# Gated mix of a spectral filter and a diagonal recurrence on one core: recurrence by token chunks, transforms split by parity, skip and gate on the matrix engine

## The chip, the cores and the metric

The kernel runs on 1 core of one Trainium2 chip. The time is the device time of one execution, in microseconds (us). Each kernel is run several times, and the profile is one of these executions. A run is called slow here when it took over 1.5% longer than the fastest run of the same kernel; comparisons of times use fast runs. TensorE (PE) does matmuls, which accumulate in a memory called PSUM. VectorE (DVE) does the elementwise work and scans, ScalarE (ACT) moves results from PSUM to the working memory SBUF (an eviction) and computes functions, GpSimd (POOL) does small odds and ends, SyncE (SP) issues transfers (DMA).

## The reference, cut to what matters

```python
# x: 2048 tokens x 1024 features, bf16
g = sigmoid((x * gate_w).sum(-1))                       # one gate per token
a = irfft2(rfft2(x) * (w_r + 1j * w_i))                 # spectral filter
Lam_bar = exp(dt * Lam)                                 # 1024 complex states
B_bar = ((Lam_bar - 1) / Lam)[:, None] * (B_re + 1j * B_im)
for t in range(2048):
    h = Lam_bar * h + B_bar @ x[t]                      # recurrence over tokens
    b[t] = 2 * real((C_re + 1j * C_im) @ h) + x[t] * Dskip
out = g * a + (1 - g) * b
```

The kernel takes the 2-D transform apart: a d transform (a real transform over the 1024 features, by matmul with a matrix of cosines and sines), two stages over the 2048 tokens (2048 = 128 x 16, with a turn through DRAM between them), the product with w, the two token stages back (with a second turn), and the inverse d transform. The recurrence is turned into a real one: u = B x is rotated by a table of angles, scanned with a real decay on VectorE, and rotated back. In other words there are two independent branches, spectral and recurrent, whose instructions are interleaved, and a final product with C that needs both.

## The kernel before

The x loads come first. G waits behind them in SP's queue (it is issued at 17.1 us, B's first transposed load at 30.1 us), and one of the four loads of T3 is held back by a one-element copy that reads the last transposed block of x; the other loads of T3, K3, R12, JP and the columns of w are issued from 1.2 us on:

```python
    for r in range(16):
        xn = CT[r // 8][:, r % 8, :]
        nc.sync.dma_start(out=xn, in_=x[P * r:P * (r + 1), :])
    for r in range(16):
        xn = CT[r // 8][:, r % 8, :]
        pe_transpose_block(xn, xT[:, :, P * r:P * (r + 1)], nc.vector.tensor_copy)
        gjunk = stg.tile([P, D], BF16, name="gjunk", tag="stg")
        nc.vector.scalar_tensor_tensor(out=gjunk, in0=xn, scalar=1.0, in1=gw_bc, ...,
                                       accum_out=glog[:, r:r + 1])        # the gate's sum
    # ...
    T3_sb = gconst.tile([P, 16, 3, P], BF16, name="T3_sb")
    nc.gpsimd.tensor_copy(out=T3_sb[:, 0, 0, 0:1], in_=xT[:, 7, S - 1:S])
```

The recurrence goes by blocks of 128 states, each over all four chunks of 512 tokens, and writes its result to DRAM:

```python
    def pass1(jb):
        # ... transposed loads of B's block, tables of angles ...
        for c in range(NCH):
            # 16 matmuls: psu = B x for 512 tokens; u <- psu on ScalarE
            nc.vector.tensor_mul(out=cu, in0=u, in1=tab[:, 0:1, :].to_broadcast([P, 2, TC]))
            nc.vector.tensor_mul(out=su, in0=u[:, ::-1, :], in1=tab[:, 1:3, :])
            nc.vector.tensor_add(out=v, in0=cu, in1=su)
            for ri in range(2):
                nc.vector.tensor_tensor_scan(out=g[:, ri, :], data0=rb, data1=v[:, ri, :], ...)
            # ... carry to the next chunk ...
            nc.sync.dma_start(out=h_dram[c, :, jb, :, :], in_=g)
```

The d transforms contract over all 1024 features, and over all 1024 frequencies on the way back:

```python
        def fd(j):
            for h in range(2):
                for dblk in range(8):
                    nc.tensor.matmul(ps[:, K * h:K * (h + 1)], lhsT=xT_A[:, dblk, j, :],
                                     rhs=G_sb[:, dblk, K * h:K * (h + 1)], ...)
    # ... and the inverse:
            for nh in range(2):
                for c in range(2):
                    for kc in range(4):
                        nc.tensor.matmul(psy[:, 512 * nh:512 * (nh + 1)], lhsT=ZT[:, kc, c, :],
                                         rhs=Ginv_sb[:, 4 * c + kc, 512 * nh:512 * (nh + 1)], ...)
```

The last stage reads the recurrence back, rotates it, multiplies by C, and mixes on VectorE:

```python
                # 32 matmuls: ps_y = h C for 128 tokens, then
                nc.vector.tensor_mul(out=sk, in0=xc, in1=dsk_bc)                   # x * Dskip
                nc.vector.scalar_tensor_tensor(out=pre, in0=sk, scalar=omg[:, tb:tb + 1], in1=gac, ...)
                nc.vector.scalar_tensor_tensor(out=o, in0=psy, scalar=omg[:, tb:tb + 1], in1=pre, ...)
```

## Time and profile before

| | before |
|---|---|
| median of 3 runs | 508.51 us (506.78 to 509.82) |
| span of the profiled run | 507.4 us |
| PE busy | 426.4 us |
| DVE busy | 350.6 us |
| ACT busy | 183.1 us |
| mean granted TensorE clock | 0.935 |

These are lines of the profile's page of the kernel before: the span, the busy time of each engine, and the chain of work that ended last, by engine and by line. In the two lines with tile names after them, a group of instructions is given with its count, busy time, mean nanoseconds of one, and the engine's idle time just before it.

```profile
span 507.4 us, 5763 instructions
PE 426.4 (84%) x2049; PEld 211.4 (42%) x2087; DVE 350.6 (69%) x633; ACT 183.1 (36%) x246; POOL 14.0 (3%) x21
...
DVE 37%; PE 36%; DMA 10%; issue 8%; ACT 7%; SPq 1%; DVEq 0%; ACTq 0%
...
L342 PE MATMUL ps_fd<-G_sb,xT 128*128 128x512 bf16 x250 | 63.5, 408 | 15.7 <-ACT X_766 L345 7.2
...
L514 PE MATMUL ps_id<-Ginv_sb,ZT 128*128 128x512 bf16 x255 | 57.9, 380 | 1.1 <-ACT ga L519 1.0
```

The two d transforms alone, ps_fd and ps_id, are 121 of the 426 us of PE. The shares of a whole run hide that the stages have different limits, so here is the kernel before cut into stretches of time. The columns are the stretch, its length, then busy us (and instructions) of PE, PEld, DVE, ACT and POOL, the granted clock, the DMA share and GB/s.

```profile
0.00:35.35 35.35, 14.39 (x133) 12.94 (x135) 27.86 (x48) 1.28 (x1) 10.93 (x18) 0.95 1.05 231
35.35:175.00 139.65, 121.69 (x521) 64.19 (x531) 81.63 (x164) 78.09 (x125) 3.08 (x4) 0.93 0.54 118
175.00:191.80 16.80, 4.80 (x19) 1.86 (x17) 9.47 (x14) 5.31 (x10) 0.00 (x0) 0.71 1.13 237
191.80:265.00 73.20, 69.29 (x374) 30.55 (x379) 69.07 (x179) 44.90 (x51) 0.00 (x0) 0.93 0.64 194
265.00:281.00 16.00, 10.01 (x41) 5.02 (x41) 14.23 (x24) 8.95 (x13) 0.00 (x0) 0.79 0.81 142
281.00:361.00 80.00, 78.53 (x409) 40.59 (x416) 35.54 (x56) 40.17 (x45) 0.00 (x0) 1.00 0.35 117
361.00:390.00 29.00, 20.59 (x85) 8.80 (x86) 20.42 (x32) 4.39 (x5) 0.00 (x0) 0.82 0.76 273
390.00:507.40 117.40, 107.06 (x477) 47.45 (x485) 92.43 (x120) 0.00 (x0) 0.00 (x0) 0.98 0.44 154
```

Read them in order: loading and transposing x; the forward transform with the recurrence; the first turn through DRAM; the filter; the second turn; the inverse; a wait for the end of the recurrence; the product with C. In the inverse PE is busy 78.5 of 80 us, so a matmul taken away there should come off the time. In the first turn it is busy 4.8 of 16.8.

Three pieces of the chain of work, in order of time (start us, length, what), show one row block of the inverse and, just as C starts, the write of the recurrence's last result and the load of the gated branch (gac) behind it in SP's queue:

```profile
301.27 3.51 PE ps_id L514 x16
...
385.50 2.27 DMA h_scratch<-g
...
388.24 7.31 DMA gac<-ga_scratch
```

### The profile page before, as it was taken

To read this page: it belongs to the slowest core of one execution; us is meant where nothing else is said; L and a number is where in the kernel's file an instruction comes from. 1 tells how busy PE (TensorE), PEld (TensorE's weight loads), DVE (VectorE), ACT (ScalarE), POOL (GpSimd) and SP (SyncE) were. 2 spreads that over 40 slices of the span, in tenths; PEclk is the share of its full clock that TensorE was granted. 3 is DMA by queue.
4 is the path that set the end of the run, shared out by engine and by line. 5 is a ranking of instruction groups with operands and counts; after the bars stand their busy time and mean duration, and the time that the engine had idled before them with its cause. 6 is when DMAs were issued, how large, how long until landed. Compare 5 with 4: busy or idle time off the path is not lost.

```text
span 507.4 us, 5763 instructions
## 1 busy us (share of the span) xinstructions
PE 426.4 (84%) x2049; PEld 211.4 (42%) x2087; DVE 350.6 (69%) x633; ACT 183.1 (36%) x246; POOL 14.0 (3%) x21
## 2 busy tenths in 40 slices
PE   1569982999699909899995999999948979999996
PEld 1545451555264404443433445555423433444442
DVE  4993692459406956999999793003693999999842
ACT  1016762954553525368644665344310000000000
POOL 6010000000000100000000000000000000000000
PEclk9979997899799967979998999999987998999999
DMA  9999879214111796548948454431676856433311
GB/s 209 266 206 208 115 114 291 102 41 123 75 62 43 126 238 184 148 123 298 284 137 130 151 166 144 136 105 43 240 278 230 340 149 259 161 126 99 109 41 42
DMA packets 81933, 80.44 MB, mean 159 GB/s; under 512 B 46960, under 2 KB 57456, under 8 KB 81264
## 3 DMA queue, kind: packets, MB, share of 16 engines
q1 hardware_dynamic: 76384, 75.82, 51.5%
q0 software_dynamic: 5328, 3.98, 5.8%
q10 hardware_dynamic: 192, 0.27, 0.3%
q8 instruction: 16, 0.26, 0.2%
q14 instruction: 13, 0.11, 0.1%
HBM read 47.29 MB, written 28.34 MB: 149 GB/s over the span
## 4 chain that ended last, share of the span: by engine, by line
DVE 37%; PE 36%; DMA 10%; issue 8%; ACT 7%; SPq 1%; DVEq 0%; ACTq 0%
PE ps_id L514 9%; PE ps_fd L342 7%; DVE g L317 7%; PE ps_y L576 6%; PE psu L305 6%; DVE su L275 3%; DVE hch L276 3%; DVE cu L273 3%; DVE gjunk L165 2%; DVE su L312 2%; DVE cu L310 2%; DVE v L314 2%; DVE pre L586 2%; DMA turn_scratch<-A_1392 2%; DVE o L589 2%
## 5 line engine op out<-in xcount | busy, mean ns | idle before, releaser
L305 PE MATMUL psu<-xT,BTs 128*128 128x512 bf16 x495 | 121.0, 384 | 2.5 <-ACT u L308 1.6
L342 PE MATMUL ps_fd<-G_sb,xT 128*128 128x512 bf16 x250 | 63.5, 408 | 15.7 <-ACT X_766 L345 7.2
L576 PE MATMUL ps_y<-CT_124,hch 128*128 128x512 bf16 x185 | 71.2, 385 | 5.2 <-DVE hch L276 5.2
L305 PEld LDWEIGHTS <-BTs 128*128 128x128 bf16 x512 | 50.5, 99 | 60.3 <-issue 5.5
L576 PE MATMUL ps_y<-CT_125,hch 128*128 128x512 bf16 x191 | 73.2, 384 | 0.4
L310 DVE TENSOR_TENSOR cu<-u,tab 128x1024 bf16<-128x1024 bf16 x32 | 21.7, 678 | 72.4 <-ACT u L308 71.9
L317 DVE TENSOR_TENSOR_SCAN g<-r_sb,carry,v 128x512 bf16<-128x512 f32 x48 | 59.3, 1271 | 7.9 <-DMA h_scratch<-h 7.5
L576 PEld LDWEIGHTS <-hch 128*128 128x128 bf16 x384 | 37.6, 99 | 53.0 <-DVE hch L276 7.6
L514 PE MATMUL ps_id<-Ginv_sb,ZT 128*128 128x512 bf16 x255 | 57.9, 380 | 1.1 <-ACT ga L519 1.0
L342 PEld LDWEIGHTS <-xT 128*128 128x128 bf16 x256 | 37.4, 146 | 41.0 <-issue 23.3
L308 ACT CAST u<-psu 128x1024 bf16<-128x1024 f32 x32 | 32.4, 1012 | 42.1 <-PE psu L305 35.2
L514 PEld LDWEIGHTS <-ZT 128*128 128x128 bf16 x256 | 25.1, 98 | 32.8 <-issue 4.7
L589 DVE SCALAR_TENSOR_TENSOR o<-ps_y,omg,pre 128x1024 bf16<-128x1024 f32 x16 | 20.4, 1278 | 17.0 <-PE ps_y L576 17.0
L576 PE MATMUL ps_y<-CT_124,hch_3418 128*128 128x512 bf16 x61 | 24.4, 399 | 8.1 <-DMA hch_3418<-h_scratch 8.1
L519 ACT ACTIVATE ga<-ps_id,gA 128x1024 bf16<-128x1024 f32 x16 | 17.8, 1112 | 34.5 <-issue 22.2
L576 PE MATMUL ps_y<-CT_125,hch_3418 128*128 128x512 bf16 x64 | 25.5, 399 | 0.3 <-issue 0.2
L576 PEld LDWEIGHTS <-hch_3418 128*128 128x128 bf16 x128 | 13.0, 102 | 25.3 <-DMA hch_3418<-h_scratch 8.6
L273 DVE TENSOR_TENSOR cu<-gch,tab_3452 128x1024 bf16<-128x1024 bf16 x24 | 16.4, 683 | 9.0 <-DMA gch<-h_scratch 8.9
L314 DVE TENSOR_TENSOR v<-cu,su 128x1024 bf16<-128x1024 bf16 x32 | 21.9, 685 | 0.3
L312 DVE TENSOR_TENSOR su<-u,tab 128x1024 bf16<-128x1024 bf16 x32 | 21.9, 683 | 0.0
L149 PE MATMUL pt<-ident,CT_124 128*128 128x128 bf16 x64 | 7.5, 311 | 15.7 <-DVE xT L150 9.3
L586 DVE SCALAR_TENSOR_TENSOR pre<-sk,omg,gac 128x1024 f32<-128x1024 bf16 x16 | 20.4, 1276 | 0.1
(651 smaller groups left out, 548.2 us busy)
## 6 DMA issues: line engine op xcount, KB each, us to landing
h_scratch<-g SPq DMA_DIRECT2D x24, 256.0 KB, 2.7
gch<-h_scratch SPq DMA_DIRECT2D x3, 2048.0 KB, 8.5
Bb<-turn_scratch SPq DMA_DIRECT2D x16, 256.0 KB, 3.8
Cq<-turn_scratch SPq DMA_DIRECT2D x16, 256.0 KB, 2.9
ga_scratch<-ga SPq DMA_DIRECT2D x16, 256.0 KB, 3.2
xc<-in_A_x_dram SPq DMA_DIRECT2D x16, 256.0 KB, 2.7
gac<-ga_scratch SPq DMA_DIRECT2D x16, 256.0 KB, 2.7
out_dram<-o SPq DMA_DIRECT2D x16, 256.0 KB, 2.0
```

The lines of the kernel that those rows point to most:

```text
L273: nc.vector.tensor_mul(out=cg, in0=g_in, in1=tab2[:, 0:2, :])
L305: nc.tensor.matmul(psu[:, ri, :], lhsT=BTs[:, ri, dblk, :], rhs=xT[:, dblk, TC * c:TC * (c + 1)], start=(dblk == 0), stop=(dblk == 7))
L308: nc.scalar.copy(out=u, in_=psu)
L310: nc.vector.tensor_mul(out=cu, in0=u, in1=tab[:, 0:1, :].to_broadcast([P, 2, TC]))
L312: nc.vector.tensor_mul(out=su, in0=u[:, ::-1, :], in1=tab[:, 1:3, :])
L314: nc.vector.tensor_add(out=v, in0=cu, in1=su)
L317: nc.vector.tensor_tensor_scan(out=g[:, ri, :], data0=rb, data1=v[:, ri, :], initial=(0.0 if carry is None else carry[:, ri:ri + 1]), op0= ...
L342: nc.tensor.matmul(ps[:, K * h:K * (h + 1)], lhsT=xT_A[:, dblk, j, :], rhs=G_sb[:, dblk, K * h:K * (h + 1)], start=(dblk == 0), stop=(dblk ...
L514: nc.tensor.matmul(psy[:, 512 * nh:512 * (nh + 1)], lhsT=ZT[:, kc, c, :], rhs=Ginv_sb[:, 4 * c + kc, 512 * nh:512 * (nh + 1)], start=(i == ...
L576: nc.tensor.matmul(psy[:, 512 * dh:512 * (dh + 1)], lhsT=hch[:, jb, ri, P * tq:P * (tq + 1)], rhs=CT[ri][:, jb, 512 * dh:512 * (dh + 1)], ...
L586: nc.vector.scalar_tensor_tensor(out=pre, in0=sk, scalar=omg[:, tb:tb + 1], in1=gac, op0=ALU.mult, op1=ALU.add)
L589: nc.vector.scalar_tensor_tensor(out=o, in0=psy, scalar=omg[:, tb:tb + 1], in1=pre, op0=ALU.mult, op1=ALU.add)
```

## The change

The intent is in four parts.

1. **d transforms by parity.** Even frequencies of a real sequence need only x[d] + x[d+512], odd ones only x[d] - x[d+512]. With the sums made once on VectorE, each d transform has 8 matmuls of 512 columns per row block in place of 16. The inverse forms even and odd parts, and adds and subtracts them on VectorE.
2. **Recurrence by chunks of tokens.** All eight blocks of chunk 0 come first, then chunk 1, and so on. The result h stays in SBUF until the product with C reads it, so the round trips of h and of the tables through DRAM go, and C of early chunks can start before the recurrence is over. B is read again for each chunk. Pairs of blocks share VectorE instructions of 2048 elements per partition.
3. **Skip and gate on PE.** x * Dskip becomes a product with diagonal matrices, accumulated into the PSUM of C; the gate's sum becomes a product with gate_w.
4. Constants in layouts that load contiguously, tables with fewer rows, and pools that reuse memory. The copies of transposed x move from VectorE to ScalarE.

The core of the diff, cut:

```diff
-            for h in range(2):
-                for dblk in range(8):
-                    nc.tensor.matmul(ps[:, K * h:K * (h + 1)], lhsT=xT_A[:, dblk, j, :], ...
+            for cls in range(2):
+                for d4 in range(4):
+                    nc.tensor.matmul(ps[:, cls, :], lhsT=preT_A[:, cls, d4, j, :], rhs=G_sb[:, cls, d4, :],
+                                     start=(d4 == 0), stop=(d4 == 3))
...
+        nc.vector.tensor_add(out=preT[:, 0, :, sl], in0=xT[:, 0:4, sl], in1=xT[:, 4:8, sl])
+        nc.vector.tensor_sub(out=preT[:, 1, :, sl], in0=xT[:, 0:4, sl], in1=xT[:, 4:8, sl])
...
+            for cls in range(2):
+                for i in range(4):
+                    nc.tensor.matmul(psy[:, cls, :], lhsT=ZT[:, 4 * cls + i, :], rhs=Gi_sb[:, 4 * cls + i, :], ...
+            eo = gt.tile([P, 2, K], BF16, name="eo", tag="gx3")
+            nc.scalar.activation(out=eo, in_=psy, func=ACT.Copy, scale=gA[:, bp:bp + 1])
+            nc.vector.tensor_add(out=ga[:, 0], in0=eo[:, 0], in1=eo[:, 1])
+            nc.vector.tensor_sub(out=ga[:, 1], in0=eo[:, 0], in1=eo[:, 1])
...
+                for d4 in range(4):                      # in the product with C: the skip
+                    d8 = 4 * dh + d4
+                    nc.tensor.matmul(psy[:, P * d8:P * (d8 + 1)], lhsT=xT[:, d8, P * tb:P * (tb + 1)],
+                                     rhs=dgD[:, d8, :], start=False, stop=(d4 == 3))
...
+    for r in range(4):
+        load_x(r)
+    fetch_BT(0, 0)                                       # transposes B, writes it back to DRAM
+    for r in range(4):
+        turn_x(r)
+        load_x(r + 4)
+    chunk_x(0)
...
+    fft["G"] = pre.tile([P, 2, 4, K], BF16, name="G_sb")
+    nc.sync.dma_start(out=fft["G"], in_=cG)              # nothing holds these back
+    fft["T3"] = t3p.tile([P, 16, 3, P], BF16, name="T3_sb")
+    nc.scalar.dma_start(out=fft["T3"], in_=cT3)
...
+    for c in range(NCH):
+        for q in range(4):
+            for j in range(2):
+                # fetch the next B block; make tables in chunk 0
+                b_gemm(c, jb, u[:, j])
+            ssm(c, q, u, h)                              # h stays in SBUF
+            # c == 0: pull the forward transform; c == 1: load C, pull the filter and inverse;
+            # c == 2: C of chunks 0 and 1; c == 3: C of chunk 2; C of chunk 3 follows
```

## The prediction

> **What bounds the kernel now.** No single engine over the 507 us (page: PE busy 84%, DVE 69%, ACT 36%). Busy time by windows gives stages: start to 35 us (DVE 28, PE 14); forward transform 35-175 (PE 122 of 140); turn through DRAM 175-192 (PE 5); filter 192-265 (PE 69, DVE 69 of 73); second turn 265-281 (PE 10); inverse 281-361 (PE 79); wait for the recurrence 361-390 (PE 21); product with C 390-507 (PE 107, DVE 92). So mostly PE, with about 80 us of PE idle at the start, the turns and before C. The chain of waits agrees: DVE 37%, PE 36%, DMA 10%.
>
> **Costs.** In the C stage 49 matmuls of 512 columns take 10.74 us on the chain: 219 ns each. PE work falls from about 1824 such units to 1632: d transforms lose 256, skip and gate add 32 each. That is 42 us.
> DVE: a bf16 tensor-tensor of 1024 takes 0.68, of 512 0.42, so 2048 about 1.21 (estimate; the Trainium skill, "VectorE: DVE Perf Modes", tier table, has 1224 ns; these two durations have its slope). The gate reduction (16 x 1.2), sk (10.9), pre (20.4) and xT copies (10.3) go; preT (8 x 1.2) and parity sums (16 x 0.84) come. The recurrence costs 4 x 1.21 + 4 x 0.68 + 4 x 1.27 = 12.6 us per pair of blocks, 202 in all, as before. DVE about 313, from 351.
> ACT takes the xT copies and loses two table rows per block: about 205, from 183. Round trips of h and tables go; B^T is reread per chunk (12 MB), about even.
>
> **On the critical path, by stage (estimates, from the new instruction order).**
> - Start: ACT does 16 xT copies and five tables before the first transform is evicted; transforms flow near 59 us (before 40).
> - Chunk 0 with the forward transform: ACT-bound (35 us of evictions, 16 tables, 6 u, with ACT and DVE waiting on each other), ends near 130; before 175.
> - Chunk 1 with the filter: DVE-bound (51 recurrence + 35 filter + 5 fixup), DMA near full since the C transposes fall here: ends near 232, before 258.
> - Second turn unhidden; inverse starts near 249.
> - Inverse: eight matmuls, eviction, next eight. Before 4.87 us per row block (3.41 + 1.46); now 1.71 + 1.46 = 3.2: 51 us, saves 27. Ends at 300.
> - C of chunks 0 and 1, PE-bound, 7.8 us per tile with the skip: 362. DVE catches up with chunk 2 under it. The 29 us wait before C vanishes.
> - Chunk 3 with C of chunk 2: PE 14.8 and DVE 13.9 per pair, 59 us: 421.
> - C of chunk 3: 31, a stall of 3 for the last h, tail 4: about 458.
>
> **Predicted: 456 us**, 8 in 10 between 430 and 485 (before 508.5; ratio 0.90). Faster by over 2%: 0.95; within: 0.04; slower: 0.01.
>
> **What would show it.** ps_id groups of 8 at about 3.2 us pitch; no gap over 5 us between the last ps_id and the first ps_y; PE idle in the first 60 us larger than before; DVE over 85% busy in the filter stage, PE under 85%; 219-225 ns per ps_y matmul; PE busy about 370, DVE 313, ACT 205.
>
> **What would make it wrong.** ACT and DVE interlock in chunk 0 worse than assumed (a table waiting behind a 12 us recurrence), so the forward stage ends at 145; the C transposes delay the filter's loads by over 10 us; DVE falls behind in chunk 3, so the recurrence's tail is exposed before the last C (up to +15). Faster: the start flows earlier, or the filter's DVE work begins during chunk 0 (to 435).

## The result, and the profile after

The time fell from 508.11 to 463.96 us (medians of 4 runs each on the same chip; 508.2 and 460.0 by the means of the fast runs). The four runs of the changed kernel took 458.46, 461.54, 466.38 and 470.37 us; the last two count as slow, and the profiled run is the one of 466.38. The ratio of fast runs is 0.9052 (95% interval 0.8981 to 0.9122). A ratio is the mean time of one kernel's fast runs over the mean of the other's of the same rounds, so it is not quite the ratio of the medians that are quoted. The granted clock of the four runs lies between 0.966 and 0.972, with the slowest run at 0.972, so the slow runs are not explained by it.

The same lines of the page, after; the group of pt is the transposing of x, that of psu the product with B:

```profile
span 464.6 us, 5250 instructions
PE 378.8 (82%) x1958; PEld 185.3 (40%) x1993; DVE 289.4 (62%) x420; ACT 191.8 (41%) x251; POOL 5.9 (1%) x11
...
PE 36%; DVE 14%; DMA 9%; issue 5%; ACT 4%; SPq 3%; ACTq 0%; DVEq 0%
...
L276 PE MATMUL psu<-xT,BTs 128*128 128x512 bf16 x498 | 121.2, 384 | 15.1 <-DMA BTs<-bt_scratch 14.0
...
L165 PE MATMUL pt<-ident,xn 128*128 128x128 bf16 x128 | 11.6, 254 | 31.9 <-DMA xn<-in_A_x_dram 26.3
...
L326 PE MATMUL ps_fd<-G_sb,preT 128*128 128x512 bf16 x125 | 29.9, 379 | 3.9 <-ACT X_684 L329 1.0
L489 PE MATMUL ps_id<-Gi_sb,ZT 128*128 128x512 bf16 x126 | 29.9, 378 | 3.1 <-ACT eo L492 3.0
```

The d transforms fell from 121 to 60 us of PE. But the transposing of x now has 26 us of PE waiting for x's loads ahead of it. Stretches of time, after (start; forward transform with chunk 0; first turn; filter with chunk 1; second turn; inverse; all of C with chunks 2 and 3):

```profile
0.00:75.00 75.00, 33.28 (x208) 18.27 (x211) 23.91 (x59) 39.68 (x61) 5.87 (x11) 0.93 0.74 138
75.00:145.50 70.50, 63.87 (x281) 33.07 (x286) 53.12 (x64) 62.98 (x93) 0.00 (x0) 1.00 0.52 160
145.50:155.00 9.50, 7.88 (x35) 3.31 (x35) 6.80 (x12) 3.30 (x6) 0.00 (x0) 1.00 0.88 234
155.00:242.00 87.00, 70.32 (x387) 29.96 (x391) 81.95 (x145) 40.53 (x45) 0.00 (x0) 0.96 0.88 241
242.00:258.50 16.50, 11.11 (x49) 5.10 (x49) 6.39 (x6) 3.11 (x5) 0.00 (x0) 0.80 0.69 144
258.50:306.40 47.90, 44.66 (x254) 25.02 (x258) 10.99 (x29) 30.45 (x31) 0.00 (x0) 1.00 0.49 165
306.40:464.60 158.20, 147.69 (x754) 70.57 (x767) 106.20 (x110) 11.73 (x14) 0.00 (x0) 0.97 0.22 77
```

PE idle time (length less busy) by stage, worked out from the two tables:

| stage | before | after |
|---|---|---|
| start, to the first evicted transform | 21.0 | 41.7 |
| forward transform | 18.0 | 6.6 |
| first turn | 12.0 | 1.6 |
| filter | 3.9 | 16.7 |
| second turn | 6.0 | 5.4 |
| inverse | 1.5 | 3.2 |
| wait and C | 18.8 | 10.5 |
| sum | 81.0 | 85.8 |

So between these two profiles the span fell by 42.8 us, PE's busy time by 47.6 us, and PE's idle time did not fall at all: the idle time that the new order took out of the forward transform, the first turn and the wait before C came back at the start and in the filter. (A trace lacks some matmul records, here under 2% in both, counted by the weight loads beside them. That makes both sums of idle time too large by at most about 8 us, alike.)

One caution: the profile before is of a fast run, the profile after of a slow one, 6.4 us above the fast mean. A fast profile with the same start exists, that of e_double_d below. There the first transform is evicted at 70.5 us, and PE is idle for 34.6 us until then, 7.1 less than here. With that start the right column would add up to 78.7 us (an estimate from these numbers), beside 81.0: the reading stands, but the start is somewhat less late than this profile shows it.

Two pieces of the chain show the shortened inverse, one row block every 3.1 us:

```profile
262.29 1.78 PE ps_id L489 x8
...
265.38 1.78 PE ps_id L489 x8
```

The waits of the start, 0 to 75 us (who waited for whom, us in total, times, longest):

```profile
PE pt L165 <- DMA xn<-in_A_x_dram: 26.3, 3, 22.3
ACT xT L166 <- PE pt L165: 20.6, 1, 20.6
DVE Wc_f L378 <- DMA Wc<-in_A_w_i_dram: 17.8, 1, 17.8
```

And the transfers issued in the first 40 us (KB each, us from issue to landing):

```profile
xn<-in_A_x_dram SPq DMA_DIRECT2D x9, 256.0 KB, 3.8
T_sb<-c_T ACTq DMA_DIRECT2D x1, 1536.0 KB, 27.0
G_sb<-c_G SPq DMA_DIRECT2D x1, 1024.0 KB, 28.5
```

The constants T_sb and G_sb (T3 and G in the code) are under way while x is loading: G no longer stands behind all of x in SP's queue, and no copy holds any part of T3. B's transposed loads have moved to the front as well. In the first 36 us the DMA engines are busy 1.02 of the time and move only 138 GB/s; before, they were as busy at the start (1.05) and moved 231 GB/s. SP's queue holds, in this order: one transposed load of B, three loads of x, the other transposed load of B, G_sb, the write of B's block (which waits 25.5 us for its transposes to land), and only then the fourth load of x, the one that PE waits for.

Two questions are left. Which part of the change made the gain? And what made the start late: SP being held by the write of B, or the constants filling the DMA engines?

### The profile page after: what moved, and what is told of

The parts are those of the page before. It is cut to its first block, busy times and chain, and to the rows that moved or that the text cites. A ratio compares the mean times of both kernels' runs of the same rounds, so it can differ in the third digit from the quotient of the medians.

```text
span 464.6 us, 5250 instructions
## 1 busy us (share of the span) xinstructions
PE 378.8 (82%) x1958; PEld 185.3 (40%) x1993; DVE 289.4 (62%) x420; ACT 191.8 (41%) x251; POOL 5.9 (1%) x11
## 4 chain that ended last, share of the span: by engine, by line
PE 36%; DVE 14%; DMA 9%; issue 5%; ACT 4%; SPq 3%; ACTq 0%; DVEq 0%
PE ps_y L547 15%; PE psu L276 11%; DVE g L294 5%; PE ps_id L489 5%; DMA BTs<-bt_scratch 4%; DMA Bb<-turn_scratch 2%; ACT eo L492 2%; DVE o L556 2%; DVE pb L302 2%; PE ps_fd L326 1%; DMA W_b<-in_A_w_r_dram 1%; PE ps_y L551 1%; SPq L653 1%; DMA W_b<-in_A_w_i_dram 1%; DVE pa L301 1%
## 5 line engine op out<-in xcount | busy, mean ns | idle before, releaser
L547 PE MATMUL ps_y<-CT_1199,h 128*128 128x512 bf16 x250 | 96.2, 385 | 5.6 <-DVE o L556 5.1
L547 PE MATMUL ps_y<-CT_1200,h 128*128 128x512 bf16 x250 | 96.2, 385 | 0.3
L547 PEld LDWEIGHTS <-h 128*128 128x128 bf16 x512 | 49.6, 99 | 61.2 <-issue 8.3
L294 DVE TENSOR_TENSOR_SCAN g<-r_sb,carry,v 128x512 bf16<-128x512 f32 x48 | 58.4, 1266 | 0.0
L556 DVE SCALAR_TENSOR_TENSOR o<-ps_y,omg,gac 128x1024 bf16<-128x1024 f32 x16 | 20.5, 1279 | 37.4 <-PE ps_y L551 37.4
L494 DVE TENSOR_TENSOR ga<-eo 128x512 bf16<-128x512 bf16 x16 | 6.8, 425 | 47.9 <-ACT eo L492 47.9
L326 PE MATMUL ps_fd<-G_sb,preT 128*128 128x512 bf16 x125 | 29.9, 379 | 3.9 <-ACT X_684 L329 1.0
L489 PE MATMUL ps_id<-Gi_sb,ZT 128*128 128x512 bf16 x126 | 29.9, 378 | 3.1 <-ACT eo L492 3.0
L285 DVE TENSOR_TENSOR v<-u,tab 128x2048 bf16<-128x2048 bf16 x16 | 19.6, 1223 | 16.0 <-ACT u L278 15.8
L326 PEld LDWEIGHTS <-preT 128*128 128x128 bf16 x128 | 18.5, 144 | 15.3 <-issue 6.2
L166 ACT COPY xT<-pt 128x1024 bf16<-128x1024 bf16 x16 | 15.3, 1007 | 20.6 <-PE pt L165 20.6
L301 DVE TENSOR_TENSOR pa<-g,tab 128x2048 bf16<-128x2048 bf16 x16 | 19.6, 1224 | 0.4
L286 DVE TENSOR_TENSOR su<-u,tab 128x2048 bf16<-128x2048 bf16 x16 | 19.5, 1219 | 0.0
L302 DVE TENSOR_TENSOR pb<-g,tab 128x2048 bf16<-128x2048 bf16 x16 | 19.5, 1218 | 0.0
```

Source lines behind the costliest of these rows:

```text
L285: nc.vector.tensor_mul(out=v, in0=u, in1=tab[:, js, 0:1, :].to_broadcast(sh))
L294: nc.vector.tensor_tensor_scan(out=g[:, j, ri, :], data0=rb, data1=v[:, j, ri, :], initial=(0.0 if c == 0 else carry[:, jb, ri:ri + 1]), o ...
L301: nc.vector.tensor_mul(out=pa, in0=g, in1=tab[:, js, 2:3, :].to_broadcast(sh))
L302: nc.vector.tensor_mul(out=pb, in0=g[:, :, ::-1, :], in1=tab[:, js, 3:4, :].to_broadcast(sh))
L326: nc.tensor.matmul(ps[:, cls, :], lhsT=preT_A[:, cls, d4, j, :], rhs=G_sb[:, cls, d4, :], start=(d4 == 0), stop=(d4 == 3))
L489: nc.tensor.matmul(psy[:, cls, :], lhsT=ZT[:, 4 * cls + i, :], rhs=Gi_sb[:, 4 * cls + i, :], start=(i == 0), stop=(i == 3))
```

## The experiments

All are correct to the reference's tolerance unless said otherwise. "The fast mean" is the mean of a kernel's fast runs; that of the changed kernel is 460.0 us, that of the kernel before 508.2 in the rounds of the result. The experiments ran later, on three chips, with the kernel before: its fast means there were 507.6, 507.4 and 506.1 us.

### e_wclate: the small loads of w held back

Theory at the start: the four loads of single columns of w, element by element, clog the DMA engines. They are made to wait for the last block of x.

```diff
         Wc = t3p.tile([P, 16, 4], BF16, name="Wc")
+        nc.gpsimd.tensor_copy(out=Wc[:, 0, 0:1], in_=xT[:, 7, S - 1:S])
+        ... (the same for 1:2, 2:3, 3:4)
```

> The new kernel with one thing moved: the four loads of two columns of W, 2 bytes an element, are issued after x is transposed, not at 2 us. Theory B (these element-wise loads hold the DMA engines, so the first B transposes land only at 32 us, and the x loads queued behind them wait): the first transposed B block lands before 15 us, the 22 us gap of PE before the fourth x block shrinks under 8, total 440 to 450 (fast runs of the new kernel are 458 to 462). Theory A (the queue is blocked by the write of B to DRAM, whatever makes the transposes slow) without B: gap stays over 15 us, total within 4 us of the new kernel.

Measured: 482.05 us median (481.59 to 484.61), ratio 0.9506. It became slower by 23 us than the changed kernel by fast means, and neither theory's numbers held. The longest x gap was 17.0 us in place of 22.3, but the 22.3 is of the slow profile; in the fast profile with the same start (e_double_d) it was 13.1. The copy of the fourth block of x started at 31.6 us here and at 31.2 there, so holding back w's columns alone brought x no earlier. And VectorE works in order and its cast Wc_f stands early in its stream: it now waited 20.7 us for w at one stretch, until 83.4 us. Tables and transforms behind it came late, and the first transform was evicted at 89.5 us. The run's time is confounded by that wait. What follows: a load that is held back must have no early reader on an in-order engine.

### e_btpool: the write of B off SP's queue

```diff
-            nc.sync.dma_start(out=bt_dram[jb], in_=BTs)
+            nc.gpsimd.dma_start(out=bt_dram[jb], in_=BTs)
```

> The new kernel with the writes of transposed B to DRAM issued from the GpSimd queue, so that no x load stands behind one. Theory A (in-order queue: x loads wait behind this write): the PE gap before the fourth x block falls from 22 us to under 8, even if the transposes land late, and the total falls by 12 to 20 us to 440 to 448. Rival: the start has slack, as ScalarE's copies and tables bound it: gap closes, total falls by under 6.

Measured: 468.62 us median (462.89 to 473.68), ratio 0.9194; no gain (6.7 us more than the changed kernel by fast means). The wait of 25.5 us left SP's queue, as it must, but PE's longest wait for x stayed at 23.9 us and the first transform was evicted at 79.8 us. B's second transposed load landed only at 27.7 us, and SP spent 20.9 us in issuing two loads of x. So the blocking write looks like a symptom: what is issued in this stretch is slow. This run's time is confounded, too: the write now stood in GpSimd's queue before the loads of w's columns, which were issued at 28.4 us in place of 1.7, and VectorE waited 29.9 us for them.

### e_gate: the constants wait for x

```diff
-    nc.sync.dma_start(out=fft["G"], in_=cG)
+    seen = xT[:, 7, P * 10 - 1:P * 10]
+    nc.gpsimd.tensor_copy(out=fft["G"][:, 0, 0, 0:1], in_=seen)
+    nc.gpsimd.dma_start(out=fft["G"], in_=cG)
...                                                      (T3, K3, R12, JP in the same way; w as in e_wclate)
-            Wc_f = ...; nc.vector.tensor_copy(out=Wc_f, in_=Wc)
+            Wc_f = ...; nc.gpsimd.tensor_copy(out=Wc_f, in_=Wc)
```

> The new kernel with the constants of the transforms (2.7 MB) and the columns of W issued from the GpSimd queue behind a one-element copy that waits for the tenth (for W the last) transposed block of x, and the cast of the W columns moved from VectorE to GpSimd; the write of transposed B still stands before x loads. Theory C (the constants' traffic, which before held back by such a copy, takes the DMA engines ahead of x): first transposed B block lands before 12 us, gap of PE before the fourth x block falls from 22 us to under 8, first transform evicted near 58 instead of 70-76, total 442 to 450. Rival (the order of the traffic does not matter, the transposes are slow): gap over 15 us, total within 5 us of the new kernel, 458 to 470. Second rival (late constants delay the first transform): gap closed, transform not earlier than 70.

Measured: 456.14 us median (452.05 to 458.45), ratio 0.8984. The start did what the theory says: PE's longest wait for x fell from 22.3 to 6.7 us (13.1 in the fast profile of e_double_d), and the first transform was evicted at 55.2 in place of 75.6 us (70.5 in e_double_d). These are ScalarE's copy of the fourth block of x and its first eviction (x2 is a group of two), in the changed kernel, in e_double_d and in e_gate:

```profile
37.91 1.01 ACT L166 COPY xT<-pt 128x1024 bf16<-128x1024 bf16 x1 [20.59 <-PE pt L165]
75.56 1.30 ACT L329 CAST X_613<-ps_fd 128x1024 bf16<-128x1024 f32 x1
...
31.23 1.01 ACT L166 COPY xT<-pt 128x1024 bf16<-128x1024 bf16 x1 [13.16 <-PE pt L165]
70.54 1.33 ACT L329 CAST X<-ps_fd 128x1024 bf16<-128x1024 f32 x1
...
17.21 1.01 ACT L166 COPY xT<-pt 128x1024 bf16<-128x1024 bf16 x1 [4.65 <-PE pt L165]
55.17 2.44 ACT L329 CAST X<-ps_fd 128x1024 bf16<-128x1024 f32 x2
```

From the copy to the eviction it is 37.7, 39.3 (with eight more matmuls, 1.8 us) and 38.0 us. So the whole difference at the start is the arrival of that block of x; the cast that e_gate also moved off VectorE made none. (e_gate also issues the constants from GpSimd's queue; the old queues with late constants were not tried.)

But only 4.3 us of these 20 (15 against e_double_d) reached the end: 455.7 against 460.0 by fast means, where the theory had 442 to 450. From the first eviction on, the forward stage took 76 us in place of 66, and VectorE waited 16.3 us at one stretch for a table row from ScalarE. The likely reason is that ScalarE now had the copies of x, the tables and the transforms' evictions closer together; the next run tests it. A wait at one engine had turned into a wait at the next.

### e_gate_split: as e_gate, with every second copy of x on VectorE

```diff
-        nc.scalar.copy(out=xT[:, :, P * r:P * (r + 1)], in_=pt)
+        (nc.scalar.copy if r % 2 == 0 else nc.vector.tensor_copy)(out=xT[:, :, P * r:P * (r + 1)], in_=pt)
```

> As e_gate, and every second PSUM copy of transposed x on VectorE instead of ScalarE (8 x 0.68 us in place of 8 x 1.0). Theory (with x in time, ScalarE's copies and tables bound the start): another 5 to 9 us off, total 434 to 444. Rival (ScalarE is not the limit, or the following stage is bound by it anyhow): within 3 us of e_gate.

Measured: 445.02 us median (442.99 to 453.22), ratio 0.8760 (0.8722 to 0.8798). This beats both kernels: 15.7 us less than the changed kernel by fast means, and 11.4 less than e_gate, more than the 5 to 9 us expected. The first transform is evicted at 51.2 us, and the forward stage takes 70 us. The transfers of the first 40 us in its profile:

```profile
xn<-in_A_x_dram SPq DMA_DIRECT2D x16, 256.0 KB, 2.8
T_sb<-c_T POOLq DMA_DIRECT2D x1, 1536.0 KB, 9.0
G_sb<-c_G POOLq DMA_DIRECT2D x1, 1024.0 KB, 5.9
```

The same two constants that took 27.0 and 28.5 us beside x, the transposes of B and the columns of w now land in 9.0 and 5.9 us, and all 16 loads of x are issued in this time. The transfers were not made smaller; they were kept apart. This agrees with what the Trainium skill states in "DMA: Bandwidth & Descriptors", section "Issuing engines are not separate DMA queues": transfers of all issuing engines run on the same 16 DMA engines and interleave, and another issuing engine saves the sequencer's time alone. It fits e_btpool's failure, too. The table in the section "Bandwidth" of the same page has 6.15 us for 1 MB issued from GpSimd, as the engines' busy span without the issuing; 5.9 us from issue to landing is near it, so little delayed this transfer. The 28.5 us were for the same 1 MB issued from SP beside the other traffic.

### b_half_d: the kernel before, with half of the d transforms' matmuls left out

Wrong (relative error 0.0243). It does the first part of the change alone, without the parity sums that it costs VectorE.

```diff
-                for dblk in range(8):
+                for dblk in range(4):
...
-                for c in range(2):
+                for c in (nh,):
```

> The kernel before with half of the matmuls of the two d transforms left out (wrong result on purpose): the parity split's matmul count alone, without its sums. Theory (most of the gain of the change is the halved transforms): inverse stage 80 to 52, forward stage 140 to 115-122, total 460 to 470. Rival (the time is given back in the wait for the recurrence before C, as VectorE's chain sets it): that wait grows from 29 by 10 to 30 us, total 476 to 495.

Measured: 454.69 us median (454.39 to 458.03), ratio 0.8972. That is 52.2 us less than before by the fast means (455.4 against 507.6), of 256 matmuls x 0.219 us = 56 us that were taken away, and more than the theory expected. From the first to the last eviction the forward transform took 106 us in place of 129, and the matmuls of the inverse 55 in place of 80. So in the kernel before, work of PE in these two stages is passed on almost in full. The rival was that the time comes back in the wait for the recurrence before C; from the last inverse matmul to the first of C there were 25 us here and 22 before.

### e_double_d: the changed kernel with both d transforms done twice

```diff
-            for cls in range(2):
+            for cls in (0, 1, 0, 1):
```

(in both transforms; the second pass starts the accumulation anew, so the result is right.)

> The new kernel with every matmul of the two d transforms done twice (same result): the matmul count of before in these two places, 256 more, 56 us at 219 ns. If both stages pass it on: inverse pitch 3.1 to 4.9 us, inverse stage 48 to 76, forward stage 70 to 90-98, total 502 to 516. Rival (the forward stage is bound by ScalarE and hides it): inverse passes on 28, forward under 10, total 488 to 498.

Measured: 521.61 us median (518.11 to 532.65), ratio 1.0252 (1.0197 to 1.0308). It is 60 us above the changed kernel by fast means, a little more than the 56 us put in and than the 502 to 516 us expected, and slower than the kernel before (520.4 against 507.6). So with as many transform matmuls as before, the rest of the change costs 13 us net. That rest still has what the parity split costs VectorE and ScalarE (sums and interleaved evictions). Together with b_half_d this answers the first question: the halved transforms make the whole gain, and more.

### e_skip_dve and e_best1: the skip back on VectorE

The 128 matmuls with diagonal matrices go; x's rows are loaded again, multiplied by Dskip and added on VectorE. e_skip_dve changes the changed kernel, e_best1 changes e_gate_split.

```diff
-                for d4 in range(4):
-                    d8 = 4 * dh + d4
-                    nc.tensor.matmul(psy[:, P * d8:P * (d8 + 1)], ..., rhs=dgD[:, d8, :], ...)
+            xc = fin["p"].tile([P, D], BF16, name="xc")
+            nc.sync.dma_start(out=xc, in_=x[P * tb:P * (tb + 1), :])
...
+            nc.vector.tensor_mul(out=xc, in0=xc, in1=dsk_bc)
+            nc.vector.scalar_tensor_tensor(out=gac, in0=xc, scalar=omg[:, tb:tb + 1], in1=gac, ...)
```

> The new kernel with x * D back on VectorE as before (0.68 + 1.28 us per tile) and without the 128 small matmuls. Theory (after the inverse PE is the limit and the 8 small matmuls cost 0.86 us per tile, 14 us in all; VectorE has room under the first eight tiles and the last four, but not in chunk 3): the part from the end of the inverse to the end 158 to 147-152, total 6 to 11 us below the new kernel, 449 to 455. Rival (VectorE's extra 1.96 us per tile makes chunk 3 bound by it: 15.9 against 14.0 per pair): no gain or a loss, within 3 us.

Measured for e_skip_dve: 462.46 us median, but of six runs three were fast (457.59, 457.6, 458.09) and three slow (466.83, 481.6, 490.64); ratio 0.9021. The fast mean, 457.8 us, is 2.3 less than that of the changed kernel: within 3 us, as the rival has it. The profiled run is slow and its start is even later (x turned only by 75 us), so its whole span says nothing. Its stretch from the end of the inverse to the end, 160.7 us against 158.2, suggests that taking 128 matmuls from PE gained nothing there; the fast profile of e_best1 has to confirm it.

> e_gate_split and e_skip_dve together. If the two gains are in separate stages, they add: total 425 to 437. If e_skip_dve gives nothing, this is within 3 us of e_gate_split.

Measured for e_best1: 452.13 us median (448.61 to 454.97), ratio 0.8910; 7.6 us more than e_gate_split by fast means, outside both expectations. After the inverse it took 160.4 us against 156.8, and in chunk 3 the step from one tile's last VectorE operation to the next tile's became 15.8 us on average in place of 14.2: nearly the rival's 15.9. PE lost 128 matmuls and the stage became longer, so in chunk 3 VectorE sets the pace once it has the skip. (The rest of the 7.6 us lies outside this stretch and is not explained.) The skip belongs on PE.

### e_best_again, e_best_noskip, e_best_double: three runs on another chip

The first is e_gate_split once more, as a yardstick.

> The same kernel as e_gate_split, once more, as the yardstick of this call: 441 to 453 us, ratio to the kernel before 0.870 to 0.885. Outside of that, the comparison of the two other runs with it needs care.

Measured: 445.83 us median (439.77 to 447.39), ratio 0.8819 (0.8776 to 0.8863); it repeats, at the upper end of what was expected for the ratio. Two of its four runs count as slow.

e_best_noskip leaves the skip's matmuls out with nothing in their place (wrong; relative error 0.998).

```diff
-                                     rhs=CT[ri][...], start=(i == 0), stop=False)
-                for d4 in range(4):
-                    ... (the skip's matmuls)
+                                     rhs=CT[ri][...], start=(i == 0), stop=(i == 15))
```

> Wrong on purpose: the 128 matmuls of the skip are left out, so x times D is missing from the output. Theory (TensorE bounds everything from the inverse to the end, so what the skip costs it is passed on in full): about 0.86 us less per tile of tokens in all 16 tiles, 431 to 434 us against 445. Rival (under chunk 3 VectorE's recurrence sets the pace, so the skip costs nothing in the 8 tiles that overlap chunks 2 and 3): 438 to 440 us.

Measured: 438.90 us median (437.04 to 442.99), ratio 0.8683; 6.9 us less by medians, but only 2.6 less by the means of the fast runs (439.5 against 442.0). The median is the rival's number, but my theory had the size of the skip wrong, and this has to be set right before the two are compared. The stretch from the end of the inverse to the end, first of e_best_again, then of e_best_noskip:

```profile
282.70:438.00 155.30, 145.89 (x770) 69.71 (x768) 106.32 (x110) 11.73 (x14) 0.00 (x0) 0.99 0.23 78
```

```profile
288.70:436.10 147.40, 138.90 (x642) 62.33 (x639) 105.93 (x110) 11.73 (x14) 0.00 (x0) 1.00 0.24 82
```

The 128 matmuls of 128 columns are 145.89 - 138.90 = 7.0 us of PE, 0.055 us each or 0.44 per tile, not 0.86. The stretch became 7.9 us shorter (e_gate_split, the same kernel as e_best_again, has 156.8 us there, so 1.5 us can be noise), so all of it was passed on. It was passed on under chunk 3, too: there the step from one tile's last VectorE operation to the next tile's is 13.8 us in place of 14.3. That is the theory's mechanism with half its size. In the whole time less of it shows, since the inverse ended 6.0 us later in the profile of e_best_noskip (288.7 against 282.7), with the same code up to there. The times alone could not have told this from half of 7.0, since the runs of one kernel differ by 6 to 8 us.

e_best_double is e_gate_split with the doubled transforms of e_double_d.

> The kernel of e_gate_split with both d transforms' matmuls done twice: the rest of the change, without its halved transforms and with its start repaired. Theory (what the rest lost was the start: e_double_d lost 13 us against the kernel before, and the repair gave 19): the 57 us of the doubled matmuls are passed on, 445 + 57 = 502 us, ratio 0.98 to 0.995, so the rest becomes a small gain. Rival (the rest loses in its tail as well, and a longer forward stage hides the repaired start): 510 us or more, ratio over 1.0.

Measured: 504.37 us median (502.26 to 507.94), ratio 0.9973 (0.9919 to 1.0027). It is 504.7 us by fast means beside 506.1 for the kernel before: even. The median is 2 us above what my theory said, and the ratio lies between the ranges of the two theories (up to 0.995, and over 1.0). What follows: with a repaired start, the rest of the change neither gains nor loses; in the kernel as changed it loses about 13 us. The two repairs together, later constants and half of x's copies on VectorE, account for that (520.4 to 504.7 us); e_gate alone gave 4.3 us of it, and the moved copies without the later constants were not run.

## Why the prediction was right or wrong

**Right: the time, 456 against 463.96 us (460.0 by the fast mean), and the sum of PE's work.** The prediction had 42 us of PE work less; the trace has 47.6 us busy less, at a granted clock of 0.966 in place of 0.935. (Its list of signs has PE busy about 370 us, which is more than 42 less; it was 378.8.) Span and busy time fell nearly alike.

**Right: the inverse.** Predicted 51 us at a pitch of 3.2; measured 47.9 us at 3.1. The first matmul of C follows the last of the inverse at once (306.2 and 306.4 us), so the wait of 29 us before C did vanish.

**Right: the filter is bound by VectorE with the DMA engines near full.** DVE is busy 82 of 87 us, PE 70, the DMA share is 0.88. The prediction called the exchange of traffic "about even". In bytes it is better than that (80 MB to 67 MB), but PE's groups show 14.0 us of waiting for the reread blocks of B.

**Mis-sized: the start.** The step was "Start: ACT does 16 xT copies and five tables before the first transform is evicted; transforms flow near 59 us". It was 75.6 us (70.5 in the fast profile of e_double_d). The prediction counted ScalarE's work there and took x as present; in fact PE waited 26 us for x (22 in e_double_d). With the constants held back (e_gate), the first eviction came at 55.2, near the predicted 59. The cause is shown by three runs, told by when ScalarE copied the fourth block of x: at 39.0 us with a freed queue (e_btpool) and at 31.6 with w's columns alone held back (e_wclate), against 31.2 with neither (e_double_d); but at 17.2 with the constants held back as well (e_gate). So w's columns alone are not it. Which of the five constants matters, and whether B's transposes beside them are needed for the harm, is not taken apart.

**How the error shrank on its way.** The forward stage ended at 145.5 for 130 predicted, 15 us late. The prediction had named 145 as the sign of ScalarE and VectorE blocking each other, but from the first eviction on the stage took 70 us for 71 predicted: it was late because its start was. Then the filter ended at 242 for 232; the inverse began at 258.5 for 249 and ended at 306.4 for 300; the first half of C ended at 367.7 for 362; the end came at 464.6 for 458. The filter with its turn took 96.5 us for 102 predicted, the inverse 48 for 51, which left 6 us of the error at the end. That these two stages made up for half of the late start was not foreseen; that part of the agreement is luck. A part of what is left may be the profiled run itself, which is one of the two slow ones: it is 6.4 us above the fast mean.

**VectorE's sum: right durations, set beside another measure.** 313 us were predicted and 289.4 were busy, although single instructions had the predicted durations: the Trainium skill gives 1224 ns for a bf16 tensor-tensor of 2048 elements ("VectorE: DVE Perf Modes", the tier table), and the four such groups of the recurrence have means of 1218 to 1224 ns. Two of them, and the scans:

```profile
L301 DVE TENSOR_TENSOR pa<-g,tab 128x2048 bf16<-128x2048 bf16 x16 | 19.6, 1224 | 0.4
L302 DVE TENSOR_TENSOR pb<-g,tab 128x2048 bf16<-128x2048 bf16 x16 | 19.5, 1218 | 0.0
...
L294 DVE TENSOR_TENSOR_SCAN g<-r_sb,carry,v 128x512 bf16<-128x512 f32 x48 | 58.4, 1266 | 0.0
```

Consecutive instructions overlap a little, and busy time counts an overlap once: 48 scans of 1266 ns are 60.8 us, busy for 58.4. Added one by one, the durations of all VectorE instructions in the trace are 317.4 us, near the predicted 313 (393.0 before, where 350.6 were busy). The prediction started from a busy time and added and subtracted durations.

**Not said in the prediction: that most of the change pays for nothing.** It told the 29 us before C as a saved wait, but PE was busy for 20.6 of them. After the inverse, PE has 147.7 us of work in place of 127.7 (the two last rows of before together), because chunk 3's product with B and the skip now fall there, and its idle time fell from 18.8 to 10.5. So the stretch became longer, 158.2 for 146.4 us. A wait filled with work that had been done elsewhere for free is a gain only if that elsewhere becomes shorter, and there the start and the filter took it back.

## What to carry to other kernels

Add up idle time and busy time of the limiting engine by stage, before and after: where a change moves work between stages, only the two sums tell whether a vanished wait was won or moved. Constants that depend on nothing are issued early and compete with the first input for the same DMA engines; hold them back with a small dependence on the input, take care that no early instruction of an in-order engine reads them, and look at which engine is the next limit (here ScalarE's copies, half of which went to VectorE). To size one part of a change, double it in the new kernel and halve it in the old one, before arguing about the rest.

## What the Trainium skill lacked or had wrong

- "TensorE: Matmul & The Clock Gate", section "Back-to-back issue gap", has a sustained 131 ns for each matmul of 512 columns with its weight load, and about 216 ns as an isolated gap. No stretch here shows 131: in the chain before, 16 matmuls took 3.51 us, 219 ns each; after, 8 took 1.78 us, 223 ns each, with no wait in between. For 128 columns it has 81 ns sustained and about 56 isolated; the skip's matmuls, each with its own weight load, cost 55 ns of PE's busy time by the difference of e_best_again and e_best_noskip.
- "DMA: Bandwidth & Descriptors", section "Bandwidth", gives times of single transfers by size. No page has a figure for mixed traffic: 1 MB took 28.5 us to land beside transposed loads, single-column loads and other constants (21.7 in the fast profile of e_double_d), and 5.9 us when kept apart from them and issued from GpSimd.
- No page has the cost of an eviction from PSUM on ScalarE that interleaves its bf16 output (step of two elements): 1.28 to 1.38 us for 128x1024 after (ps_fd), where the contiguous one before takes 0.99 to 1.01 us.
